# A mixture-of-experts kernel: both products of an expert in matmul pairs of 64 rows, and other rules for the list scheduler

## The chip, the cores and the metric

The kernel runs on one core of a Trainium2 chip. The metric is the time of one execution on the device, in microseconds; of several executions the median counts. TensorE multiplies (its weight loads are listed apart, as PEld), VectorE (DVE) and ScalarE (ACT) compute elementwise, GpSimd (POOL) issues the indirect DMAs, SyncE (SP) issues the other DMAs.

## What is computed

A causal convolution with 7 taps, whose weights are a softmax for each of 8 heads, runs over `x` of 8 x 3584 x 192. Its output rows, 28672 tokens of 192, go through a layer of 8 experts, of which each token takes the two with the largest noisy logits:

```python
logits = x @ w_gate
noise_scale = np.log1p(np.exp(x @ w_noise))
noisy_logits = logits + noise_scale * noise
top2 = np.argpartition(-noisy_logits, 2, axis=1)[:, :2]
...
h = np.maximum(x[mask] @ w1[e], 0.0)
out[mask] += top2_w[mask, k, None] * (h @ w2[e])
```

`w1` is 192 x 1024 and `w2` 1024 x 192 for each expert; the weights of the two experts are a softmax over their two logits. All is float32.

## The kernel before

The tokens are worked on in 28 units of 1024 (8 for each of 128 partitions). For a unit, `conv` makes the convolution on VectorE (56 instructions `tensor_scalar` and `scalar_tensor_tensor`, L560 and L562; for the first five units TensorE does it, L514), scales the rows by a power of two and splits each number into two float16, high and low part, in the tile `rb`. `gating` computes the logits with 24 small matmuls (L637), picks the two experts on VectorE, ranks the tokens of each expert with two more matmuls (L721, L723) or nine in the first units, and `scatters` writes each row to its place in its expert's region of a buffer `xs` in DRAM, by 16 indirect DMAs of GpSimd (L768).

The experts then work in rounds: the first takes 128 rows of each expert, the other 28 take 256. So there are 232 blocks, 224 of them with 256 rows. Each block is loaded by two transposing DMAs into `bT` (three buffers). The first product (`mm1`, L848) has its result, 1024 x 256, in two halves `ph` of two PSUM banks each (two buffers). As the operands are pairs of float16, a product is high x high, high x low and low x high. The rows 128 to 191 of the 192 fill only 64 rows of TensorE. High and low part of these stand side by side on 128 partitions for two of the three products; for the third, low weight with high data, `mm1` runs matmuls of 64 rows, two at a time, on the two halves of the array. For each half that makes 16 matmuls of 128 rows and 4 of 64. Half 0 has its short ones last, half 1 first:

```python
todo = full + todo if half == 0 else todo + full
```

`relu` (ScalarE, L854) writes the high part of the result to `h`, `relu_low` (VectorE, L858) its low part, after which the banks are free. The second product (`mm2`, L866) runs for the block ahead, in two halves of 128 rows with 24 matmuls each, into `py` (one bank each, two buffers). `scaled` (ScalarE, L872) multiplies by the gate, and `add_rows` (GpSimd, L877) adds the rows to the output by an indirect DMA, once the adds of the block ahead have landed.

The order of the instructions on each engine is fixed when the program is built. Each task is a generator that yields an engine and a number of microseconds, and `Plan.run` always takes the task with the smallest `at - urge`, where `at` is the time at which it could start by the plan's own clock. `Ring` holds the number of free buffers, `Mark` makes a task wait for another. `due(u)` says when a unit must be scattered by the plan. `ready_unit` says how many units must be scattered before a round's rows are there: the mean number of rows less 3 standard deviations. The engines run their queues strictly in this order; what they wait for is set by semaphores.

## Time and profile before

| | us |
|---|---|
| median of three runs | 2117.39 |
| the three runs | 2103.3, 2119.4, 2117.39 |
| the profiled execution | 2097.99 |
| its span, first to last instruction | 2096.2 |
| in it: TensorE busy | 1983.7 |
| VectorE busy | 1565.0 |
| GpSimd busy | 1271.8 |
| ScalarE busy | 803.3 |

The profile shows one execution. Busy times of engines overlap, so they don't add up to the span. A line number is one of the kernel. In the timeline a row is a stretch of like instructions on one engine: start and length in microseconds, what is written from what, how many, and in brackets how long the engine was idle ahead of it and what ended that. "issue" is a time in which it waited for nothing that the profile shows. A matmul's length is from its start to its modelled end; matmuls overlap, so the rate is read from the starts.

### The profile page before, as it was taken

The page shows a single profiled execution, that of the slowest core. Times are in us where ns is not written, and L with a number is a line of the kernel's source. Part 1 is how long each engine was busy: PE and PEld are TensorE (multiplying, and loading weights), DVE is VectorE, ACT ScalarE, POOL GpSimd, SP SyncE. Part 2 cuts the span into 40 slices and gives each one's busy share as a digit, 9 for nine tenths or more (in the row PEclk, how much of TensorE's full clock was granted, in tenths as well). Part 3 has the DMA queues.
Part 4 walks back from the last instruction along what each step waited for, and adds up shares of the span by engine and source line. Part 5 has one row for each costly group of instructions (what it writes and reads, how often), then busy time and mean ns, then how long its engine had stood idle before and what let it go on. Part 6 is the DMA issues. An engine that isn't in the chain of part 4 may idle for free.

```text
span 2096.2 us, 52494 instructions
## 1 busy us (share of the span) xinstructions
PE 1983.7 (95%) x21703; PEld 1778.0 (85%) x21703; DVE 1565.0 (75%) x4042; ACT 803.3 (38%) x1173; POOL 1271.8 (61%) x915
## 2 busy tenths in 40 slices
PE   7557999999999999999999999999999999999997
PEld 6546888878888899889899998988898888999986
DVE  6677888878888898889988888889899753333232
ACT  4334343333334343443343434433443433333332
POOL 0353576765666776777667777777767665333333
PEclk9778999999999999999999999999999999999999
DMA  8733456876657677666777766677777664444442
GB/s 238 196 91 79 86 98 118 155 148 118 117 92 125 130 132 128 122 126 117 118 129 133 126 130 117 113 120 131 130 132 115 107 98 77 58 61 57 60 58 35
DMA packets 521882, 236.99 MB, mean 113 GB/s; under 512 B 401304, under 2 KB 508824, under 8 KB 521505
## 3 DMA queue, kind: packets, MB, share of 16 engines
q1 hardware_dynamic: 433824, 142.72, 33.2%
q0 software_dynamic: 87200, 90.80, 29.3%
q8 instruction: 171, 2.80, 0.6%
q14 instruction: 79, 0.65, 0.1%
q10 hardware_dynamic: 608, 0.02, 0.0%
HBM read 40.12 MB, written 115.38 MB: 74 GB/s over the span
## 4 chain that ended last, share of the span: by engine, by line
PE 88%; DVE 5%; issue 3%; SPq 2%; ACT 1%; DMA 1%; another core or an unknown queue 0%; ACTq 0%; POOL 0%; DVEq 0%; POOLq 0%
PE ph L848 43%; PE py L866 41%; PE ph L514 1%; SPq L622 1%; PE misc L637 1%; DVE h L858 1%; PE grams L364 1%; DVE xc L562 0%; DMA xT<-rb 0%; DVE w1s L412 0%; SPq L911 0%; DVE w2s L412 0%; PE py L613 0%; DVE t L673 0%
## 5 line engine op out<-in xcount | busy, mean ns | idle before, releaser
L877 POOL DMA_INDIRECT out_dram<-y,ids x456 | 776.0, 1702 | 593.2 <-ACT y L872 423.5
L848 PE MATMUL ph<-bT,w1s 128*128 128x256 f16 (+2 forms) x9280 | 1004.7, 273 | 26.6 <-issue 10.3
L866 PE MATMUL py<-w2s,h 128*128 128x192 f16 x10944 | 953.1, 246 | 12.0 <-issue 11.3
L848 PEld LDWEIGHTS <-w1s 128*128 128x128 f16 (+1 forms) x9280 | 773.2, 98 | 210.6 <-issue 116.6
L866 PEld LDWEIGHTS <-h 128*128 128x128 f16 x10944 | 910.0, 98 | 23.8 <-issue 18.3
L858 DVE SCALAR_TENSOR_TENSOR h<-ph,h 128x1024 f16<-128x1024 f32 (+1 forms) x464 | 557.5, 1203 | 389.8 <-ACT h L854 345.2
L854 ACT ACTIVATE h<-ph 128x1024 f16<-128x1024 f32 (+1 forms) x464 | 468.0, 1009 | 556.8 <-PE ph L848 469.1
L768 POOL DMA_INDIRECT xs<-rb,idx x448 | 494.2, 1103 | 212.7 <-issue 144.7
L562 DVE SCALAR_TENSOR_TENSOR xc<-xt,wt,xc 128x192 f32<-128x192 f32 x1224 | 422.9, 410 | 3.3 <-DMA xt<-zero 3.3
L872 ACT ACTIVATE y<-py,ga 128x192 f32<-128x192 f32 x456 | 191.5, 421 | 602.2 <-PE py L866 439.2
L514 PE MATMUL ph<-xt,dg 128*128 128x192 f32 x280 | 50.8, 339 | 14.9 <-DMA xt<-in_x_dram 11.6
L514 PEld LDWEIGHTS ph<-xt,dg 128*128 128x128 f32 x280 | 47.3, 197 | 15.3 <-DVE dg L494 11.5
L560 DVE TENSOR_SCALAR xc<-xt,wt 128x192 f32<-128x192 f32 x204 | 53.9, 330 | 1.2 <-DMA xt<-in_x_dram 0.5
L575 DVE TENSOR_REDUCE am<-xc 128x8 f32<-128x1536 f32 x28 | 49.0, 1752 | 4.4 <-ACT xc L569 3.7
L579 DVE TENSOR_TENSOR xc<-xc,xs 128x1536 f32<-128x1536 f32 x28 | 49.3, 1761 | 0.0
L637 PE MATMUL misc<-gparts,xT 128*128 128x32 f16 (+1 forms) x752 | 27.4, 175 | 16.7 <-issue 15.3
L673 DVE SCALAR_TENSOR_TENSOR t<-t,t 128x64 f32<-128x64 f32 x168 | 38.1, 227 | 5.7
L637 PEld LDWEIGHTS <-xT 128*128 128x128 f16 x752 | 24.4, 97 | 19.8 <-issue 17.6
L589 DVE TENSOR_TENSOR rb<-xc,rb 128x1024 f16<-128x1024 f32 x28 | 34.1, 1217 | 4.3 <-ACT rb L585 2.1
L585 ACT ACTIVATE rb<-xc 128x1024 f16<-128x1024 f32 x28 | 29.5, 1053 | 11.1 <-DVE xc L579 9.3
L483 ACT ACTIVATE xt<-xt 128x1152 f32<-128x1152 f32 x27 | 31.2, 1156 | 0.0
L719 DVE TENSOR_REDUCE sums<-M 128x72 f16<-128x576 f16 x23 | 27.0, 1172 | 0.0
(142 smaller groups left out, 620.0 us busy)
## 6 DMA issues: line engine op xcount, KB each, us to landing
out_dram<-zero SPq DMA_DIRECT2D x28, 768.0 KB
xt<-in_x_dram SPq DMA_DIRECT2D x27, 768.0 KB
bT<-xs SPq DMA_TRANSPOSE x464
out_dram<-y,ids POOLq DMA_INDIRECT x456
xs<-rb,idx POOLq DMA_INDIRECT x448
w2s<-in_moe_w_dram SPq DMA_DIRECT2D x16, 384.0 KB
w1s<-in_moe_w_dram SPq DMA_DIRECT2D x8, 512.0 KB
w1s<-in_moe_w_dram SPq DMA_DIRECT2D x16, 256.0 KB
```

The source lines that it names most:

```text
L514: nc.tensor.matmul(c[:, h - h0, :TU * G].rearrange("p (t g) -> p t g", g=G), diag[h, k], xts[u][:, k:k + TU, h * G:(h + 1) * G], start=(k ...
L560: V.tensor_scalar(dst, src, wt[:, h, k:k + 1], None, op0=OP.mult)
L562: V.scalar_tensor_tensor(dst, src, wt[:, h, k:k + 1], dst, op0=OP.mult, op1=OP.add)
L579: V.tensor_tensor(xc, xc, xsc[:, :, None].to_broadcast([P, TU, D]), op=OP.mult)
L637: nc.tensor.matmul(lg[:, t], xT[:, t, c, :], g[:, gc], start=(i == 0), stop=(i == len(seq) - 1))
L768: s = nc.gpsimd.indirect_dma_start(out=xsf, out_offset=bass.IndirectOffsetOnAxis(ap=idx[:, k, t:t + 1], axis=0), in_=rbf[:, t, :], in_offs ...
L848: nc.tensor.matmul(ph[:, f, :T], w, x, start=f // 2 not in banks[:i], stop=f // 2 not in banks[i + 1:], skip_group_check=True)
L854: nc.scalar.activation(h[:, 0, half * nf:(half + 1) * nf, :T], ph[:, :, :T], AF.Relu)
L858: V.scalar_tensor_tensor(h[:, 1, hs, :T], ph[:, :, :T], 0.0, h[:, 0, hs, :T], op0=OP.max, op1=OP.subtract)
L866: nc.tensor.matmul(py[:, :D], h[:, a, f, ts], w2_part(e, lo, f), start=(n == 0), stop=(n == 3 * FC - 1))
L872: nc.scalar.activation(y, py[:, :D], AF.Copy, scale=gate)
L877: a = nc.gpsimd.indirect_dma_start(out=out, out_offset=bass.IndirectOffsetOnAxis(ap=ids, axis=0), in_=y, in_offset=None, compute_op=OP.add)
```

## The change

Both products are cut into matmuls of 64 rows. One on rows 0 to 63 and one on rows 64 to 127 form a pair that writes two different banks. `mm1_pairs` makes two passes over a half: in the first, rows 0 to 63 add to the first bank and rows 64 to 127 to the second, in the second pass (`swap`) the other way round. The matmuls which had 64 rows before are part of the first pass. `mm2_pairs` does the same with the two halves of 128 rows of a block. The first pass has 20 matmuls for each half of the first product, the second 16; the second product has 48 in each pass. `passes` puts a no-op on ScalarE that waits for the last matmul of a first pass, and the first matmul of the second pass waits for it.

The order of a block's work on TensorE is now: first pass of the first product, both halves; first pass of the second product for the block ahead; second pass of the first product, both halves; second pass of the second product for the block ahead. Both `py` banks are held through it. Rounds of 128 rows keep `mm2` as it was.

The scheduler counts 0.3 us more for what follows TensorE (`DRAIN`), and when the best task leaves its engine idle till then, it takes another that ends before (the loop over `able`). Numbers of the plan change: `ready_unit` takes 2.2 standard deviations, the logits of units from the sixth on are planned 5.0 us after their transposes (2.5 before), a scatter takes 1.4 us and an add 2.0, and scatters are due 5 us earlier.

```diff
+    DRAIN = 0.3
...
+                gap = 0.0 if th[4] == eng else self.GAP + (self.DRAIN if th[4] == "PE" else 0.0)
+                at = max(self.clock[eng], th[0] + gap)
...
+            for one in able:
+                if one[2][1][0] == best[2][1][0] and one[1] + one[2][1][1] <= best[1]:
+                    if one[0] < best[0] or one[1] < best[1]:
+                        best = one
...
-            if mean * (u + 1) - 3.0 * sigma * math.sqrt(u + 1) >= end:
+            if mean * (u + 1) - 2.2 * sigma * math.sqrt(u + 1) >= end:
...
-                yield plan.now + 2.5
+                yield plan.now + 5.0
...
-                yield DVE, 0.7
+                yield DVE, 1.1
                 sums = small.tile([P, TU + 1, E], F16, name="sums")
...
+                yield plan.now + 1.0
                 yield PE, 0.1
...
-            yield POOL, 1.05
+            yield POOL, 1.4
...
-            slack = (due(u) - 40.0 - plan.now) / (2 * TU - i)
+            slack = (due(u) - 45.0 - plan.now) / (2 * TU - i)
             if u > 1:
-                yield plan.now + min(2.0, max(0.0, slack - 1.0))
+                yield plan.now + min(2.6, max(0.0, slack - 1.4))
...
+    def passes(what, mm):
+        yield ACT, 0.1
+        passed[what] = nc.scalar.nop()
+        needs(passed[what], mm)
+        done("passed", what, mm.ins.name)
+
+    ROWS = [slice(64 * i, 64 * i + 64) for i in range(2)]
+
+    def mm1_pairs(e, xT, T, half, swap, ph):
+        nf = FC // 2
+        bank = [(f, f + nf // 2) if not swap else (f + nf // 2, f) for f in range(nf // 2)]
+        todo = []
+        for fs in bank:
+            for lo, wc, c in [(0, 0, 0), (1, 0, 0), (0, 0, 1), (0, 1, 2)]:
+                todo += [(f, w1_part(e, wc, lo, half * nf + f)[r], xT[r, c, :T]) for f, r in zip(fs, ROWS)]
+            if not swap:
+                todo += [(f, w1_part(e, 1, 1, half * nf + f)[r], xT[r, 2 + i, :T])
+                         for i, (f, r) in enumerate(zip(fs, ROWS))]
+        for i, (f, w, x) in enumerate(todo):
+            mm = nc.tensor.matmul(ph[:, f, :T], w, x, start=not swap and i < 2, stop=swap and i >= len(todo) - 2,
+                                  skip_group_check=True)
+            if swap and i == 0:
+                needs(mm, passed["ph"])
+        return mm
+
+    def mm2_pairs(e, h, swap, pys):
+        todo = [(i, f, a, lo) for f in range(FC) for a, lo in ((0, 0), (0, 1), (1, 0)) for i in range(2)]
+        for n, (i, f, a, lo) in enumerate(todo):
+            t = 1 - i if swap else i
+            mm = nc.tensor.matmul(pys[t][:, :D], h[ROWS[i], a, f, t * P:(t + 1) * P], w2_part(e, lo, f)[ROWS[i]],
+                                  start=not swap and n < 2, stop=swap and n >= len(todo) - 2, skip_group_check=True)
+            if swap and n == 0:
+                needs(mm, passed["py"])
+        return mm
...
-            for half in range(2):
-                yield PE, 0.1 + 1.96 * T / BIG, ph_ring
+                yield PE, 1.09 * T / BIG, ph_ring
+                phs.append(psum.tile([P, FC // 2, BIG], F32, name="ph", bufs=2))
...
+                mm = mm1_pairs(e, xTs[n], T, half, False, phs[half])
+            plan.spawn(passes("ph", mm), 1.5)
+            if n:
+                yield from second(n - 1, False)
+            yield mark("passed", "ph", mm.ins.name)
+            for half in range(2):
+                yield PE, 0.88 * T / BIG
+                mm1_pairs(e, xTs[n], T, half, True, phs[half])
+                plan.spawn(evacuate(n, half, phs[half], T), 1.5)
...
-                yield from second(n - 1)
-        yield from second(len(blocks) - 1)
+                yield from second(n - 1, True)
+        for swap in (False, True):
+            yield from second(len(blocks) - 1, swap)
```

What this does to the order of the instructions is shown at three places. On VectorE, in the middle of the program, the low parts of `h` (from `ph`) before stood one at a time between steps of the convolution (`xc`):

```order
L858 SCALAR_TENSOR_TENSOR h<-ph,h 128x1024
L562 SCALAR_TENSOR_TENSOR xc<-xt,wt,xc 128x8x24 x11
L858 SCALAR_TENSOR_TENSOR h<-ph,h 128x1024
L562 SCALAR_TENSOR_TENSOR xc<-xt,wt,xc 128x8x24 x2
L858 SCALAR_TENSOR_TENSOR h<-ph,h 128x1024
L562 SCALAR_TENSOR_TENSOR xc<-xt,wt,xc 128x8x24 x14
L858 SCALAR_TENSOR_TENSOR h<-ph,h 128x1024
```

In the same stretch of a later unit they now stand in pairs, one pair for each block, here too with the convolution between them:

```order
L567 TENSOR_SCALAR xc<-xt,wt 128x8x24
L903 SCALAR_TENSOR_TENSOR h<-ph,h 128x1024 x2
L567 TENSOR_SCALAR xc<-xt,wt 128x8x24 x7
L569 SCALAR_TENSOR_TENSOR xc<-xt,wt,xc 128x8x24 x11
L903 SCALAR_TENSOR_TENSOR h<-ph,h 128x1024 x2
L569 SCALAR_TENSOR_TENSOR xc<-xt,wt,xc 128x8x24 x17
L903 SCALAR_TENSOR_TENSOR h<-ph,h 128x1024 x2
```

What stood in two places of a block, 11 or 14 steps and 2 more, now stands in one, 17 or 18 steps.

On ScalarE, where a unit's gating (`t`, `lgs`) falls among the blocks, before:

```order
L854 ACTIVATE h<-ph 128x1024 x2
L872 ACTIVATE y<-py,ga 128x192
L641 ACTIVATE lgs<-misc 128x128
L662 ACTIVATE t_19894<-t_19894 128x64
L872 ACTIVATE y<-py,ga 128x192
L854 ACTIVATE h<-ph 128x1024 x2
```

And now, where the no-ops are not among the rows:

```order
L899 ACTIVATE h<-ph 128x1024 x2
L917 ACTIVATE y<-py,ga 128x192 x2
L648 ACTIVATE lgs<-misc 128x128
L669 ACTIVATE t_32533<-t_32533 128x64
L899 ACTIVATE h<-ph 128x1024 x2
```

The two results `y` of a block now stand together, and the gating stands behind them.

On TensorE, at the change from the second product to the first, with what an instruction waits for, before:

```order
L866 LDWEIGHTS h
L866 MATMUL py<-w2s_144,h 128x192
L848 LDWEIGHTS w1s_130 [waits DMAHW6_49]
L848 MATMUL ph<-bT,w1s_130 128x256 [waits DVE_49]
L848 LDWEIGHTS w1s_130
```

And now, at the change from the first pass of the second product to the second pass of the first:

```order
L891 LDWEIGHTS h
L891 MATMUL py<-w2s_152,h 128x192
L881 LDWEIGHTS w1s_136 [waits Activation_sequencer_49]
L881 MATMUL ph<-bT,w1s_136 128x256
L881 LDWEIGHTS w1s_136
```

Here a wait for ScalarE's no-op is new; the wait for VectorE stands at the first pass of each half.

More of the change, by code (lines that the diff above doesn't have):

```diff
@@ L92, in run @@
         while True:
-            best = None
+            best, able = None, []
             for th in self.threads:
@@ L97, in run @@
                 eng = th[1][0]
-                at = max(self.clock[eng], th[0] + (self.GAP if th[4] != eng else 0.0))
+                gap = 0.0 if th[4] == eng else self.GAP + (self.DRAIN if th[4] == "PE" else 0.0)
+                at = max(self.clock[eng], th[0] + gap)
                 if len(th[1]) > 2:
@@ L104, in run @@
                 urge = th[3](at) if callable(th[3]) else th[3]
+                able.append((at - urge, at, th))
                 if best is None or at - urge < best[0]:
-                    best = at - urge, at, th
+                    best = able[-1]
             if best is None:
@@ L850, in mm1 @@
         return ph
+    passed = {}
+    def passes(what, mm):
[29 more added lines that the diff above has]
+        return mm
     def relu(ph, T, half, h):
@@ L916, in round_meta @@
     def round_meta(j, mt):
-        yield plan.now + 2.3
+        yield plan.now + 4.0
         if j:
@@ L952, in results @@
             yield mark("added", n - 1)
-        yield POOL, 1.6
+        yield POOL, 2.0
         add_rows(j, ids[:, e, half:half + 1], y, adds)
@@ L956, in results, with second @@
         if half == rounds[j][1] // P - 1:
-            done("added", n, after=2.5)
-    def second(n):
+            done("added", n, after=2.8)
+    def second(n, swap):
         j, e = blocks[n]
-        for half in range(2):
-            yield mark("h", n, half)
-        adds = []
-        for half in range(rounds[j][1] // P):
-            yield PE, 2.0, py_ring
-            plan.spawn(results(n, half, mm2(e, hts[n], half), adds), 0.5)
-        hts.pop(n)
+        if swap and rounds[j][1] == P:
+            return
+        if not swap:
+            for half in range(2):
+                yield mark("h", n, half)
+        h = hts[n] if rounds[j][1] == BIG and not swap else hts.pop(n)
+        if rounds[j][1] == P:
+            yield PE, 2.0, py_ring
+            plan.spawn(results(n, 0, mm2(e, h, 0), []), 0.5)
+            return
+        if not swap:
+            pyt[n] = []
+            for half in range(2):
+                yield PE, 2.0 * half, py_ring
+                pyt[n].append(psum.tile([P, 512], F32, name="py", bufs=2))
+        else:
+            yield mark("passed", "py", turn["py"])
+            yield PE, 2.0
+        mm = mm2_pairs(e, h, swap, pyt[n])
+        if not swap:
+            turn["py"] = mm.ins.name
+            plan.spawn(passes("py", mm), 1.5)
+        else:
+            adds = []
+            for half, py in enumerate(pyt.pop(n)):
+                plan.spawn(results(n, half, py, adds), 0.5)
+    pyt = {}
     def run_blocks():
@@ L975, in run_blocks @@
             at_block[:] = n, max(plan.now, FIRST)
-            hts[n] = None
+            phs = []
             for half in range(2):
-                yield PE, 0.1 + 1.96 * T / BIG, ph_ring
+                yield PE, 1.09 * T / BIG, ph_ring
+                phs.append(psum.tile([P, FC // 2, BIG], F32, name="ph", bufs=2))
                 if half == 0:
                     hts[n] = ffn[0].tile([P, 2, FC, BIG], F16, name="h")
-                plan.spawn(evacuate(n, half, mm1(e, xTs[n], T, half), T), 0.6)
+                mm = mm1_pairs(e, xTs[n], T, half, False, phs[half])
[3 more added lines that the diff above has]
+            yield mark("passed", "ph", mm.ins.name)
+            for half in range(2):
+                yield PE, 0.88 * T / BIG
+                mm1_pairs(e, xTs[n], T, half, True, phs[half])
+                plan.spawn(evacuate(n, half, phs[half], T), 1.5)
             xTs.pop(n)
```

## The prediction

> **What bounds the kernel now.** I read the page first: busy shares, granted clock, chain of work.
>
> ```profile
> span 2096.2 us, 52494 instructions
> PE 1983.7 (95%) x21703; PEld 1778.0 (85%) x21703; DVE 1565.0 (75%) x4042; ACT 803.3 (38%) x1173; POOL 1271.8 (61%) x915
> ...
> PEclk9778999999999999999999999999999999999999
> ...
> PE 88%; DVE 5%; issue 3%; SPq 2%; ACT 1%; DMA 1%; another core or an unknown queue 0%; ACTq 0%; POOL 0%; DVEq 0%; POOLq 0%
> PE ph L848 43%; PE py L866 41%; PE ph L514 1%; SPq L622 1%; PE misc L637 1%; DVE h L858 1%; PE grams L364 1%; DVE xc L562 0%; DMA xT<-rb 0%; DVE w1s L412 0%; SPq L911 0%; DVE w2s L412 0%; PE py L613 0%; DVE t L673 0%
> ```
>
> TensorE holds 88% of the chain, nearly all in the two products, at full clock after the start. How close one block is to the rate of the array is read from the timeline, in the last stretch, where VectorE has little else to do.
>
> ```profile
> 2014.29 1.71 PEld L848 LDWEIGHTS <-w1s 128*128 128x128 f16 x16
> 2014.37 4.31 PE L848 MATMUL ph<-bT,w1s 128*128 128x256 f16 x40
> 2014.83 0.42 ACT L872 ACTIVATE y<-py,ga 128x192 f32<-128x192 f32 x1 [1.82 <-PE py L866]
> ...
> 2016.21 0.33 PEld L848 LDWEIGHTS <-w1s 64*128 64x128 f16 x8 [0.21 <-issue]
> 2016.65 1.02 ACT L854 ACTIVATE h<-ph 128x1024 f16<-128x1024 f32 x1 [1.39 <-issue]
> 2016.75 1.64 PEld L848 LDWEIGHTS <-w1s 128*128 128x128 f16 x16 [0.21 <-issue]
> 2017.70 1.22 DVE L858 SCALAR_TENSOR_TENSOR h<-ph,h 128x1024 f16<-128x1024 f32 x1 [4.81 <-ACT h L854]
> ...
> 2018.51 4.12 PE L866 MATMUL py<-w2s,h 128*128 128x192 f16 x48
> ...
> 2018.71 1.02 ACT L854 ACTIVATE h<-ph 128x1024 f16<-128x1024 f32 x1 [1.04 <-PE ph L848]
> 2019.77 1.22 DVE L858 SCALAR_TENSOR_TENSOR h<-ph,h 128x1024 f16<-128x1024 f32 x1 [0.84 <-ACT h L854]
> ...
> 2022.47 4.31 PE L848 MATMUL ph<-bT,w1s 128*128 128x256 f16 x40
> ```
>
> A block takes 2022.47 - 2014.37 = 8.10 us: 4.14 us for the first product, 3.96 us for the second. A slot of the second is 3.96/48 = 82.5 ns. Of the 16 weight loads in 1.71 us the first step is such a slot and the last takes its own 0.098 us; the 14 steps between them are 0.109 us each. The first product has 32 full matmuls and 8 of 64 rows which run two at a time, so 36 slots: 36 x 0.109 = 3.93 us. The missing 0.21 us stands in the two rows with [0.21 <-issue]: the weight loads stop where 128-row matmuls give way to 64-row ones, and again on the way back. So a block is bound by the array, and its only hole is the two changes of row mode.
>
> Then the waits of TensorE after the start, and the two loads that share its time in the middle:
>
> ```profile
> PE ph L848 <- issue: 10.3, 25, 1.2
> PE py L866 <- issue: 9.7, 23, 1.2
> PE misc L721 <- DVE sums L719: 2.2, 3, 1.3
> PE misc L637 <- DMA xT<-rb: 1.2, 2, 0.9
> ...
> 1200.00:1600.00 400.00, 397.69 (x4432) 357.63 (x4431) 354.96 (x938) 158.63 (x233) 285.93 (x204) 1.00 0.71 122
> 1600.00:1900.00 300.00, 298.09 (x3269) 269.15 (x3268) 146.38 (x303) 109.79 (x157) 163.16 (x119) 1.00 0.55 85
> ```
>
> From 200 us on TensorE waits for another engine hardly at all, but 20 us go in 48 short pauses for which the profile names no cause. VectorE (third figure) is busy 89% of the time up to about 1600 us, and half of it after.
>
> **The change, part by part.**
>
> *The pairs.* Every matmul becomes two of 64 rows on the two halves of the array, in different banks. A block then has 72 + 96 matmuls instead of 40 + 48, but in 36 + 48 slots as before, if a pair takes one slot. For that there are rows: from the first of the eight 64-row loads above to the next full one are 2016.75 - 2016.21 = 0.54 us, four slots of 0.109 us and one change of 0.1, so two of them share a slot. With half the columns or fewer, in the first blocks and the gating, the supply was tried harder:
>
> ```profile
> 163.17 0.50 PEld L848 LDWEIGHTS <-w1s 64*128 64x128 f16 x11 [0.17 <-issue]
> 44.14 1.16 PE L637 MATMUL misc<-gparts,xT 128*128 128x16 f16 x40
> ```
>
> Eight 64-row loads and three full ones in 0.50 us, and 40 matmuls with their loads in 1.16 us (29 ns each), are well over the two per 82.5 ns which the second product will ask for. So I price a slot as now, and the gain is the two mode changes: 8.10 - 36 x 0.109 - 48 x 0.0825 = 0.21 us in each of the 224 blocks of 256 rows, 48 us. In the first eight blocks, of 128 rows, the second product stays in 128-row mode, so they gain nothing.
>
> *New mode changes.* The gating's logits (24 matmuls) and its ranks (2) stay in 128-row mode and now stand between 64-row ones: for 23 of 28 units two groups, two changes each, 0.107 us a change: 9.8 us. The first five units have transposes too, about ten groups within the blocks: 2 us. Together +12 us.
>
> *The hand-over.* A second pass adds onto the banks that the other half of the array has just written, so its first load waits for a ScalarE no-op that waits for the first pass. Between the passes of the first product stand 24 slots of the second (1.98 us), and between those of the second the 16 slots of the first (1.75 us). ScalarE's longest operation here is 1.02 us, so the no-op is covered; queued behind it are only the evacuations, which need the second pass anyway. Cost 0; without cover it would be about 0.5 us a pass.
>
> *The evacuation comes closer.* Now each half's banks are needed again 6.0 us after its last matmul (the other half and all of the second product lie between). After the change the first product ends in its second passes, and only half of the second product follows before the banks are needed. From the rows: ScalarE starts 2018.71 - 2018.51 = 0.20 us after the next phase, VectorE 1.06 us later, and ends 1.22 us after that: 2.48 us. Half 0 has 8 x 0.109 + 1.98 = 2.85 us, so 0.37 us to spare. Half 1 queues behind half 0 on both engines and is done 3.63 us after half 0's last matmul; it is needed at 2.85 + 1.09 = 3.94: 0.31 us to spare. Whatever VectorE still has in hand when the ReLU is done comes off that. So what stands ahead of each pair of evacuations must fit into 7.89 us less the pair: the second frees VectorE at 2.41 + 1.14 = 3.55 us, the next pair starts at 7.89 + 1.26 = 9.15, which leaves 5.60 us, and 5.9 us with the spare. Of these the row of 14 gives the price of the filling work:
>
> ```profile
> 1252.38 1.23 DVE L858 SCALAR_TENSOR_TENSOR h<-ph,h 128x1024 f16<-128x1024 f32 x1 [0.21 <-ACT h L854]
> 1253.52 0.74 DVE L562 SCALAR_TENSOR_TENSOR xc<-xt,wt,xc 128x192 f32<-128x192 f32 x2
> ...
> 1255.59 4.69 DVE L562 SCALAR_TENSOR_TENSOR xc<-xt,wt,xc 128x192 f32<-128x192 f32 x14
> ...
> L562 DVE SCALAR_TENSOR_TENSOR xc<-xt,wt,xc 128x192 f32<-128x192 f32 x1224 | 422.9, 410 | 3.3 <-DMA xt<-zero 3.3
> ```
>
> (4.69 - 0.41)/13 = 0.33 us a step. The new order puts 17 such steps between two pairs at most: 5.6 us, just inside. The gating's groups reach about 6.2 us, but in blocks that TensorE's logits lengthen by 0.9 us. So VectorE fits by a hair; for waits inside the gating's chain I take 4 us over the run. The ends: -3.4 us, if the later logits and ranks remove the waits for L719 and the transposes, and 0.5 us in each of the 160 blocks with VectorE's work, 80 us.
>
> *Start and end.* By the order, VectorE gets 30 more convolution steps (10 us) and some routing, 18 us in all, ahead of block 16. It is busy 74 of 100 us there, as this row shows, so most fits into holes; I take +3 us, ends -5 and +18.
>
> ```profile
> 100.00:200.00 100.00, 62.11 (x695) 53.37 (x693) 74.07 (x205) 38.45 (x52) 46.29 (x39) 0.75 0.31 72
> ...
> 2084.40 1.56 POOL L877 DMA_INDIRECT out_dram<-y,ids  x1 [2.75 <-ACT y L872]
> 2086.26 1.56 POOL L877 DMA_INDIRECT out_dram<-y,ids  x1 [0.30 <-issue]
> ```
>
> At the end the last block's adds wait 2.75 us for the adds of the block ahead, not for TensorE; with both halves finishing together that wait stays. 0 us.
>
> *The pauses.* TensorE's instructions nearly double. Were the 20 us tied to their number, they would double too. But the same view from 730 us on, where two thirds of the instructions run, has 1.4 us of them left:
>
> ```profile
> PE ph L848 <- issue: 1.2, 5, 0.3
> PE py L866 <- issue: 0.2, 1, 0.2
> ...
> q8 instruction: 171, 2.80, 0.6%
> ```
>
> I take +3 us, ends 0 and +20. [...]
>
> *GpSimd, the slack of the list scheduler, the earlier readiness (2.2 for 3.0 sigma).* GpSimd is busy 286 of 400 us and off the chain; its own numbers only set where adds and scatters stand. Block loads wait for free buffers, not for scatters. 0 us, hidden by TensorE.
>
> **The sum.** -48 + 12 + 4 + 3 + 0 + 3 = -26 us. The profiled execution took 2098.0 us (span 2096.2 and 1.8 around it): 2072. But the three timed runs shown took 2103.3, 2117.4 and 2119.4, so that execution is the lowest of four, 19 us under the median. The mean of the four is 2109.5; less 26 gives 2084.
>
> **The rivals.**
>
> *A: the evacuation closes the loop, slower.* VectorE's queue is in order. If its work, or a wait in the gating, overruns the 0.31 us by 0.5 us in each of the 160 loaded blocks, TensorE loses 80 us: 2084 - 4 + 80 = 2160. It decides from 0.22 us a block (36 us net gain over 160 blocks); 1% slower from 0.36. For it speaks VectorE's 89% and that the old order kept 3.5 us of cover where the new one keeps 0.3; against it that steps on VectorE take the same time throughout.
>
> *B: the pauses follow the instruction count, no change.* 20 us more from 200 us on and as much as that again ahead of it is not excluded: 2084 - 3 + 20 = 2101, up to 2109 with a slow start.
>
> *C: supply.* TensorE must take 24 matmuls a us for milliseconds; the 40 above were a burst after which the queue could refill. If only the rate of today is sustained, 82.5 ns each, a block takes 168 x 0.0825 = 13.9 us and the kernel 3.4 ms; any rate between is possible, and the bursts are nearer. [...] No run here shows more than 40 in a row.
>
> **How the numbers follow.** About 1% (21 us) is what a measurement of this kernel can tell from no change. My forecast, 0.52: faster by more than 1%, as only the new waits above 5 us more would spoil it. B and mixtures that end within 1%: 0.31. A: 0.14. C: 0.03. The range leaves out A and C, and takes in the full 48 us and a better start from the fastest execution (2098 - 48 - 5 = 2045), and at the top B with the late start and some waits (2119 - 26 + 17 + 15 = 2125, taken as 2130).
>
> **What would show it.** In the timeline after, no [0.21 <-issue] inside a block, and blocks of 7.9 us in the last stretch; if they are 8.1, the pairs don't remove the hole. Among the waits, TensorE on VectorE's h stays under some 15 us in all; 50 us or more there is A. Issue pauses of 40 us instead of 20 are B. Slots over 90 ns in the second product are C. The forecast is wrong too if the first 16 blocks end more than 15 us later.

## The result and the profile after

The changed kernel takes 2267.57 us (four runs, 2257.89 to 2276.01), the kernel before 2114.63 in the same comparison (2103.3 to 2119.4). The ratio is 1.073, 95% interval 1.066 to 1.080: slower by 153 us, where 26 us less were forecast. The profiled execution took 2262.55 us.

Of the page after: the span, the busy shares, and the clock that was granted to TensorE in 40 slices.

```profile
span 2260.8 us, 88992 instructions
PE 2039.0 (90%) x39879; PEld 1900.0 (84%) x39879; DVE 1561.9 (69%) x4042; ACT 763.6 (34%) x1173; POOL 1310.1 (58%) x915
PEclk9677999999999999999999999999999999999999
```

VectorE is busy 3 us less than before, ScalarE 40 us less and GpSimd 38 us longer. TensorE's granted clock is 0.98 from 200 to 2080 us, where it was 1.00 before; between 200 and 800 us it is 0.95 against 0.99. TensorE is busy 90% instead of 95%. Its matmuls are 1.84 times as many. The last stretch shows what the pairs do when nothing disturbs them:

```profile
2104.11 2.08 PEld L891 LDWEIGHTS <-h 64*128 64x128 f16 x48
2106.11 2.20 PEld L881 LDWEIGHTS <-w1s 64*128 64x128 f16 x40
2108.27 1.77 PEld L891 LDWEIGHTS <-h 64*128 64x128 f16 x41
...
2110.31 0.27 PEld L891 LDWEIGHTS <-h 64*128 64x128 f16 x7 [0.27 <-issue]
```

48 loads of the second product take 2106.11 - 2104.11 = 2.00 us, 41.7 ns each, so a pair takes 83 ns; 40 of the first take 2.16 us, 54 ns each, a pair 108 ns. So in this stretch a pair takes one slot, as priced, and no change of row mode stands inside the block. But there is a pause of 0.27 us for which the profile names no cause. The waits of TensorE after 200 us (engine, line, what it waited for: us in total, times, longest) show how many of those there are:

```profile
PE py L891 <- issue: 69.5, 186, 1.1
PE ph L881 <- DVE h L903: 25.3, 52, 1.5
PE ph L881 <- issue: 18.9, 49, 1.1
PE misc L644 <- issue: 5.2, 8, 1.2
```

The 20 us of pauses before have become 94 us, mostly in the second product, and TensorE now waits 25 us for VectorE's part of `h`. These rows count only the time after the modelled end of the last matmul. Read from the starts (every step of more than 0.3 us between consecutive weight loads or matmuls for which no cause is named, after 200 us) the pauses are 38.7 us in 71 places before, and 172.5 us in 305 after. The difference, 134 us, is most of the 165 us between the two profiled executions. (Counted by what the profile names for the instruction behind each step, the pauses are 38.3 and 168.0 us, 130 us apart.)

### The profile page after: what moved, and what is told of

Read it like the earlier page. It is cut to its first block, busy times and chain, and to the rows that moved or that the text cites. A ratio compares the mean times of both kernels' runs of the same rounds, so it can differ in the third digit from the quotient of the medians.

```text
span 2260.8 us, 88992 instructions
## 1 busy us (share of the span) xinstructions
PE 2039.0 (90%) x39879; PEld 1900.0 (84%) x39879; DVE 1561.9 (69%) x4042; ACT 763.6 (34%) x1173; POOL 1310.1 (58%) x915
## 5 line engine op out<-in xcount | busy, mean ns | idle before, releaser
L922 POOL DMA_INDIRECT out_dram<-y,ids x456 | 795.2, 1744 | 700.0 <-ACT y L917 558.4
L891 PE MATMUL py<-w2s,h 64*128 64x192 f16 x21504 | 1031.1, 244 | 73.9 <-issue 69.5
L881 PE MATMUL ph<-bT,w1s 64*128 64x256 f16 (+1 forms) x16704 | 1033.3, 272 | 67.8 <-DVE h L903 30.0
L891 PEld LDWEIGHTS <-h 64*128 64x128 f16 x21504 | 921.0, 94 | 129.9 <-issue 125.0
L881 PEld LDWEIGHTS <-w1s 64*128 64x128 f16 x16704 | 884.1, 96 | 131.1 <-issue 96.4
L903 DVE SCALAR_TENSOR_TENSOR h<-ph,h 128x1024 f16<-128x1024 f32 (+1 forms) x464 | 542.3, 1202 | 494.9 <-ACT h L899 391.0
L899 ACT ACTIVATE h<-ph 128x1024 f16<-128x1024 f32 (+1 forms) x464 | 448.3, 1007 | 1002.3 <-PE ph L881 908.4
L776 POOL DMA_INDIRECT xs<-rb,idx x448 | 513.2, 1146 | 231.6 <-issue 137.5
L917 ACT ACTIVATE y<-py,ga 128x192 f32<-128x192 f32 x456 | 167.6, 419 | 213.5 <-PE py L891 150.9
L521 PE MATMUL ph<-xt,dg 128*128 128x192 f32 x280 | 50.3, 337 | 17.3 <-DMA xt<-in_x_dram 11.6
L419 DVE SCALAR_TENSOR_TENSOR w1s<-w1s,ws,w1s 128x1024 f16<-128x1024 f32 x16 | 20.6, 1285 | 10.8 <-issue 8.4
```

Source lines behind the costliest of these rows:

```text
L521: nc.tensor.matmul(c[:, h - h0, :TU * G].rearrange("p (t g) -> p t g", g=G), diag[h, k], xts[u][:, k:k + TU, h * G:(h + 1) * G], start=(k ...
L776: s = nc.gpsimd.indirect_dma_start(out=xsf, out_offset=bass.IndirectOffsetOnAxis(ap=idx[:, k, t:t + 1], axis=0), in_=rbf[:, t, :], in_offs ...
L881: mm = nc.tensor.matmul(ph[:, f, :T], w, x, start=not swap and i < 2, stop=swap and i >= len(todo) - 2, skip_group_check=True)
L891: mm = nc.tensor.matmul(pys[t][:, :D], h[ROWS[i], a, f, t * P:(t + 1) * P], w2_part(e, lo, f)[ROWS[i]], start=not swap and n < 2, stop=swa ...
L899: nc.scalar.activation(h[:, 0, half * nf:(half + 1) * nf, :T], ph[:, :, :T], AF.Relu)
L903: V.scalar_tensor_tensor(h[:, 1, hs, :T], ph[:, :, :T], 0.0, h[:, 0, hs, :T], op0=OP.max, op1=OP.subtract)
```

## Experiments

The 18 runs fell into two kinds of conditions, which the kernel before tells apart: on chips 8 and 9 it took 2040 us, on chips 4, 11 and 12 between 2110 and 2119, as in the result. On the first two there are practically no pauses in any kernel: in the eight traces from there no row of TensorE's waits after 200 us is without a cause. Each ratio is against the kernel before on the same chip; I call the two "without pauses" and "with pauses". The times expected of the first four runs (e_order_full, e_first_pairs, e_plan_only, e_relaxed) suppose pauses, and all four ran without.

### Order, planner and pairs apart (without pauses)

**e_order_full**: the changed order and planner, with full matmuls of 128 rows in the passes (the second product cut into two halves of its contraction).

```diff
-                todo += [(f, w1_part(e, wc, lo, half * nf + f)[r], xT[r, c, :T]) for f, r in zip(fs, ROWS)]
+        terms = [(0, 0, 0), (1, 0, 0)] if not swap else [(0, 0, 1), (0, 1, 2)]
+        todo = [(f, w1_part(e, wc, lo, half * nf + f), xT[:, c, :T]) for f in range(nf) for lo, wc, c in terms]
...
+        todo = [(t, f, a, lo) for f in range(FC // 2 * swap, FC // 2 * (1 + swap)) for t in range(2)
+                for a, lo in ((0, 0), (0, 1), (1, 0))]
```

> The changed kernel's order of passes, no-ops and planner, but each pass made of full matmuls of 128 rows (only the ones that were short before stay short), so TensorE has as many instructions as before the change. Rate theory (twice the instructions make TensorE pause and send its completions late): 2100 to 2150 us, issue pauses back to 20 to 50 us from 200 us on. Order theory (evacuations with 0.3 us to spare are what TensorE waits for): 2230 to 2270 us. Planner theory (the new numbers of the list scheduler): 2230 us or more.

2097.62 us, ratio 1.029 (1.025 to 1.032). But in this version the 64-row matmuls stand in two places of a block, so that it has four changes of row mode instead of two. Hence **e_order_full_2**, in which they stand side by side:

```diff
+            todo = todo + short if half == 0 else short + todo
```

> The changed order and planner with full 128-row matmuls and, unlike e_order_full, the short matmuls of both halves side by side, so two changes of row mode a block as before the change. The passes of the second product are its two halves of the contraction. Order theory: as slow against before as the changed kernel is in the same run. Pairs theory (instruction count, alone or with late completions): 0.99 to 1.015, as the kernel before has the same matmuls. If e_order_full lost its 57 us to the two more changes of mode, this kernel gains 45 to 60 us on it.

2055.86 us, ratio 1.008 (1.004 to 1.011). Two changes less in each of 224 blocks are worth 41.8 us, 0.093 us each. (The two ran on chips 9 and 8, where the kernel before took 2039.66 and 2040.95 us.) Against before, the order with the changed planner costs 15 us.

**e_first_pairs**: pairs in the first product only, in the changed order.

> The changed kernel with pairs in the first product alone; the passes of the second product are full matmuls. A block has 120 matmuls instead of 168 (before the change 88). Rate theory: the excess goes with the number, 0.4 of it or less: 2140 to 2200 us. Order theory: 2230 to 2270 us. Planner theory: 2230 us or more.

2096.86 us, ratio 1.029 (1.026 to 1.032): as e_order_full, with the same four changes of mode. It tells nothing more.

**e_plan_only**: the blocks of before in the changed planner.

> The blocks as before the change (full matmuls, old order of a block), with the changed scheduler and all its new numbers. Rate theory and order theory: 2090 to 2130 us, as before the change. Planner theory: 2230 us or more.

2045.51 us, ratio 1.001 (0.997 to 1.005). For the old blocks the planner's numbers are worth nothing there.

**e_relaxed**: all pairs, in an order that leaves each half's banks 1.46 us to spare instead of 0.3. Each half's two passes are kept together, with a pass of the second product between them.

```diff
-            for half in range(2):
-                yield PE, 0.88 * T / BIG
-                mm1_pairs(e, xTs[n], T, half, True, phs[half])
+                if half == 0 and n > 1:
+                    yield from second(n - 2, True)
+                if half == 1 and n:
+                    yield from second(n - 1, False)
...
+                yield PE, 0.88 * T / BIG
+                mm1_pairs(e, xTs[n], T, half, True, ph)
```

> All matmuls in pairs, but the passes in another order: half 0 first pass, second pass of the second product of two blocks ahead, half 0 second pass, half 1 first pass, first pass of the second product of the block ahead, half 1 second pass. By the slots each evacuation then has 1.46 us to spare instead of 0.31. Rate theory: 2220 to 2270 us, with 100 us or more of issue pauses. Order theory: 2060 to 2110 us, waits for VectorE's h under 5 us. Planner theory: 2250 us.

2029.88 us, ratio 0.995 (0.994 to 0.997): slightly faster than before. So without pauses pairs can win a little (0.5%). **after_again** is the changed kernel itself under such conditions, **e_relaxed_2** the same as e_relaxed beside it.

> The changed kernel itself, unchanged, again. In the runs above, the kernel before took 2040 us and showed no pause without a named cause, and a kernel of nothing but pairs (e_relaxed) had none either. If the 7% come from such pauses, and they belong to the conditions of the run: with pauses in the kernel before (20 us or more from 200 us on) the ratio is 1.05 to 1.08 with 150 us or more of pauses; without them it is 0.985 to 1.005, since the sum of the prediction (-26 us) holds. If the order of the passes costs the time (evacuations with 0.3 us to spare), the ratio is 1.04 or more in any run and most of it stands as TensorE waiting for VectorE's h.

> e_relaxed again, beside the changed kernel: all pairs, but each half's banks have 1.46 us to spare where the changed kernel has 0.3. If both late completions and tight evacuations are needed for the loss, this kernel keeps 0.99 to 1.01 where the changed kernel loses 3% or more; if the pauses alone make the loss, it loses as much as the changed kernel; if the run has no pauses, 0.99 to 1.00 again and the changed kernel within 1% of it.

The changed kernel took 2065.04 us, ratio 1.014 (1.010 to 1.019), above the 0.985 to 1.005 that were expected without pauses; e_relaxed_2 took 2031.89 us, ratio 0.996 (0.993 to 0.998). So of the 7% of the result 1.4% stay when the pauses are away. TensorE's waits in the changed kernel:

```profile
PE ph L881 <- DVE h L903: 19.2, 10, 10.6
...
PE py L891 <- ACT y L917: 16.1, 4, 8.2
PE misc L644 <- DMA xT<-rb: 13.5, 13, 2.0
```

and in e_relaxed_2:

```profile
PE misc L644 <- DMA xT<-rb: 10.4, 11, 2.6
...
PE py L891 <- ACT y L917: 3.1, 6, 0.5
...
PE ph L881 <- DVE h L903: 0.5, 1, 0.5
```

The two kernels are 33 us apart, and the waits for `h` and for `y` differ by 32 us. So with pairs the tight order costs some 33 us against the relaxed one: few waits, but long ones. The tight order alone does not make them. Of the next rows the first two are of e_order_full_2, which has the tight order with full matmuls, the others of e_plan_only (after 200 us), which has the order of before:

```profile
PE ph L880 <- DVE h L904: 8.0, 7, 2.5
PE py L891 <- ACT y L918: 6.7, 2, 6.5
...
PE ph L856 <- DVE h L903: 10.8, 7, 5.8
PE py L911 <- ACT y L917: 5.3, 2, 4.8
```

These two wait 15 and 16 us, the changed kernel 35 us, so the change adds some 19 us of such waits to the old blocks. Each figure is of one execution.

### What the planner has to do with it

**e_pairs_oldplan**: the changed blocks, with the planner's numbers and rules of before.

```diff
-    DRAIN = 0.3
+    DRAIN = 0.0
...
-            if mean * (u + 1) - 2.2 * sigma * math.sqrt(u + 1) >= end:
+            if mean * (u + 1) - 3.0 * sigma * math.sqrt(u + 1) >= end:
...
-            yield POOL, 1.4
+            yield POOL, 1.05
```

> The changed blocks with the planner's numbers and rules of before. Planner theory: if the changed planner costs time with pairs, this is over 1% faster than the changed kernel. If the changed planner is what keeps VectorE's work out of the way of the tight evacuations, this is 1% or more slower than the changed kernel, with the difference as waits of TensorE for h. If neither, within 0.7% of it.

2235.7 us without pauses, ratio 1.096 (1.092 to 1.101): 171 us more than the changed kernel on the same chip. VectorE's longest waits and what SyncE waits for ahead of the load `mt` (L791), then a stretch of the timeline:

```profile
DVE idf L810 <- DMA mt<-xs: 164.4, 18, 17.6
...
SPq L791 <- DMA xs<-rb,idx: 168.5, 58, 10.7
```

```profile
963.80 0.96 POOL L771 DMA_INDIRECT xs<-rb,idx  x1 [0.30 <-issue]
...
966.17 1.00 SPq L791 DMA_DIRECT2D mt<-xs  x2
...
970.23 0.19 DVE L810 COPY_PREDICATED idf<-ok,mt 128x16 f32<-128x16 int32 x1 [8.51 <-DMA mt<-xs]
...
971.37 2.35 DVE L898 SCALAR_TENSOR_TENSOR h<-ph,h 128x1024 f16<-128x1024 f32 x2
...
972.63 3.59 PE L876 MATMUL ph<-bT,w1s 64*128 64x256 f16 x34 [8.34 <-DVE h L898]
```

This is one link after the other: a unit's last scatter, then the load `mt` of a round's row numbers, which SyncE issues only once the scatters have landed, then VectorE, which has stood 8.51 us in front of that load, then the two evacuations queued behind it, then TensorE. VectorE waits for this load 18 times in the 29 rounds, 9.1 us each on average. **e_oldplan_ready** changes one number of e_pairs_oldplan, the readiness of the rounds:

```diff
-            if mean * (u + 1) - 3.0 * sigma * math.sqrt(u + 1) >= end:
+            if mean * (u + 1) - 2.2 * sigma * math.sqrt(u + 1) >= end:
```

> e_pairs_oldplan with one number of the changed planner, the 2.2 standard deviations of ready_unit. In e_pairs_oldplan VectorE waits 164 us, some 8.4 us in each round, for the round's small load of row numbers, which SyncE issues only when a unit's scatters have landed; the evacuations are queued behind it, and TensorE waits 151 us for them. Theory that the readiness of the rounds makes that wait: 2060 to 2100 us, VectorE's wait for that load under 30 us. Rival, that the planned times of scatters and adds make it: 2200 us or more, with the wait as it was.

It ran with pauses, so its 2460.51 us (ratio 1.165, 1.161 to 1.170) can't be held against the numbers expected. But the wait is gone:

```profile
DVE idf L810 <- DMA mt<-xs: 13.2, 6, 4.8
```

and TensorE's wait for `h` fell from 151.0 to 11.6 us. That the readiness made the wait is shown. How much of the 171 us it makes is not: TensorE's waits for `h` are 132 us longer in e_pairs_oldplan than in the changed kernel on the same chip, and the rest is not taken apart. Why e_oldplan_ready has 323 us of pauses, more than any other with these blocks, is open.

### The pauses

**e_start** is e_relaxed with the blocks of before, full matmuls in their order, up to block 15. **before_again** is the kernel before, on the same chip.

```diff
+    PLAIN = 16
...
+            for half in range(2) if n < PLAIN else ():
+                yield PE, 0.1 + 1.96 * T / BIG, ph_ring
...
+                plan.spawn(evacuate(n, half, mm1(e, xTs[n], T, half), T), 0.6)
```

> e_relaxed, but the first 16 blocks have the full matmuls and the order of before the change. e_relaxed was 19 us behind the kernel with before's blocks (and the changed planner) at the end of its first four blocks and 23 us at the end of the 16th. Theory that the pairs' order makes the start late: 15 to 22 us faster than e_relaxed, ratio 0.985 to 0.989. Rival, that the lost time is caught up again later since VectorE and the scatters set the middle: within 6 us of e_relaxed.

> The kernel before, unchanged, for its own profile under these conditions (2040 us in the runs above, 2115 us in those of the result). If its lower time there is due to the pauses that it lacks, TensorE's pauses without a named cause are under 5 us after 200 us instead of 20 us, and the mean step of a second-product matmul between 200 and 800 us is 82 to 84 ns instead of 85 to 91.

e_start took 2265.4 us, ratio 1.073 (1.070 to 1.076): as much as the changed kernel, with an order that has the time to spare. before_again took 2109.62 us, with 49.6 us of pauses. TensorE's waits in e_start (after 200 us):

```profile
PE py L891 <- issue: 119.0, 296, 1.3
PE ph L881 <- issue: 19.6, 57, 1.0
```

The second product (L891) asks for 24 matmuls a us and the first (L881) for 18, and they take about the same time of a block. Six times as much is lost at the faster one. By the starts e_start has 239.2 us of pauses; the 190 us more than in before_again, less the 45 us that the pairs gain, are 145 of the 152 us between the two profiled executions. Why it has more of them than the changed kernel (172.5 us) is open. What runs beside a pause shows in the timeline of e_start:

```profile
997.78 0.98 POOL L776 DMA_INDIRECT xs<-rb,idx  x1 [0.30 <-issue]
998.36 0.45 PEld L891 LDWEIGHTS <-h 64*128 64x128 f16 x9
...
999.07 0.96 POOL L776 DMA_INDIRECT xs<-rb,idx  x1 [0.30 <-issue]
...
999.26 0.17 PEld L891 LDWEIGHTS <-h 64*128 64x128 f16 x4 [0.45 <-issue]
999.98 0.22 PEld L891 LDWEIGHTS <-h 64*128 64x128 f16 x6 [0.55 <-issue]
...
1000.87 1.18 PEld L891 LDWEIGHTS <-h 64*128 64x128 f16 x29 [0.67 <-issue]
```

Two scatters of GpSimd stand one behind the other; in their time TensorE gets its loads in lumps of 4, 6, then all the rest. Over the whole run this is the rule in the kernels with pairs in the second product; in the kernel before, the pauses lie at scatters hardly more often than the share of the time would give. A table from the traces: pauses from 200 us to the last scatter, how many begin within 1.4 us of a scatter's start, and what share of the time these 1.4 us make, each counted in full.

```
kernel           pauses   within 1.4 us of a scatter   share of the time
before               71    31                            37%
after               297   214                            33%
e_start             397   352                            32%
e_start_full2       141    96                            33%
e_oldplan_ready     498   438                            26%
after the last scatter: before 0, after 8 (3.3 us), e_start 2 (0.7 us)
```

In e_start 239 of the pauses follow the one ahead by less than 1 us; the median from start to start is 0.73 us, and mostly 4 or 5 loads run between. So where TensorE pauses at a scatter it gets some 6 loads and as many matmuls a us. This is not a fixed rate that a scatter leaves over, as the next table shows. It takes the scatters between 800 and 1600 us whose first 1.4 us lie wholly within one product, what that product asks for, and the loads that TensorE started in this time:

```
kernel, product          asked a us   scatters   loads a us   scatters with a pause
before, second               12          119        12.0              2
e_start_full2, second        12           42        11.2              4
e_start_full2, first         18           51        14.6             19
e_start, first               18           29        15.0             11
after, second                24           34        12.6             26
e_start, second              24           75         9.4             69
after_again, second          24           37        24.0              0
```

In the runs with pauses, at 12 a us one is rare (6 of 161 scatters), at 18 it comes at about every third scatter (30 of 80), at 24 at most of them (95 of 109). At 24 TensorE then gets hardly more, and in e_start less, than the 12 which the old second product gets beside the same scatters. After_again, without pauses, gets all 24.

**e_start_late** plans the logits 8.0 us after their transposes.

```diff
-                yield plan.now + 5.0
+                yield plan.now + 8.0
```

> e_start with the logits planned 8.0 us after their transposes instead of 5.0. With all pairs TensorE waits 9 to 10 us in all for these transposes (13.5 us in the changed kernel, 1 to 2 us with before's blocks). If those waits are on the path: 5 to 10 us faster than e_start. If something else waits in their place (the ranks, later scatters): within 4 us of it.

2248.29 us, ratio 1.064 (1.062 to 1.067), 17 us faster than e_start; but its pauses also fell from 239 to 205 us, so the waits for the transposes are not measured by it.

**e_start_2** repeats e_start, and **e_start_full2** gives it full matmuls in the second product.

```diff
-            mm = nc.tensor.matmul(pys[t][:, :D], h[ROWS[i], a, f, t * P:(t + 1) * P], w2_part(e, lo, f)[ROWS[i]],
+            mm = nc.tensor.matmul(pys[t][:, :D], h[:, a, f, t * P:(t + 1) * P], w2_part(e, lo, f),
```

> e_start again. If before takes about 2110 us here, TensorE pauses as it did (200 to 240 us, 85 to 90% of it within 1.4 us of a scatter's start) and the ratio is 1.065 to 1.08. If before takes about 2040 us, no pauses: then the start theory says 2005 to 2017 us, 0.982 to 0.990, and its rival (the lost start is caught up) 2024 to 2034 us.

> e_start with full matmuls of 128 rows in the second product, so 12 matmuls a us there instead of 24, and pairs in the first product only. Each block has four changes of row mode, some 45 us in all. Rate theory (the queue ahead of TensorE covers an interruption at 12 to 18 matmuls a us and not at 24): in a run with pauses those at the second product fall from 119 us to under 20 us, all pauses are under 70 us, and the time is 2130 to 2170 us. Count theory (pauses in proportion to the instructions that the change adds): some 100 us of pauses, 2190 us or more. Without pauses: 2050 to 2065 us.

e_start_2: 2268.76 us, ratio 1.072 (1.069 to 1.075). e_start_full2: 2214.74 us, ratio 1.044 (1.041 to 1.048). Its waits after 200 us, ahead of them the row of the second product in e_start_2:

```profile
PE py L891 <- issue: 124.8, 315, 1.1
...
PE ph L881 <- issue: 33.5, 76, 1.1
PE ph L881 <- ACTq L864: 17.6, 25, 1.3
...
PE py L891 <- issue: 13.8, 32, 1.0
```

At the second product the pauses fell from 125 to 14 us, as the theory of the rate has it, with pairs in the first product as before; that a queue ahead of TensorE covers an interruption, as the theory puts it, no run shows. A full matmul and a pair take the same slot, 82.5 ns before and 83 ns after, so what is halved there is the number of instructions. All pauses by the starts are 84.9 us, against 238.9 in e_start_2. That is above the 70 us of the rate theory, and the time is above its range and within that of the count theory. I had left out that the first product's pauses would grow (14 to 34 us), and the no-op between the passes, for which TensorE waits 17.6 us. And I had mis-sized the changes of row mode: four in each of 216 blocks, at 0.093 us, are 80 us and not 45 against e_start, which has none there. 154 us less of pauses, 80 us more for the changes and 18 us for the no-op leave 56 us; the two kernels are 54 us apart.

**e_scatter_twice** adds a second scatter behind each, of the same rows into another buffer, from the seventh unit on, and takes the 1.4 us it needs off the plan's slack.

```diff
+            if u > 5:
+                yield POOL, 1.4
+                apart()
+                c = nc.gpsimd.indirect_dma_start(
+                    out=xs2f, out_offset=bass.IndirectOffsetOnAxis(ap=idx[:, k, t:t + 1], axis=0),
+                    in_=rbf[:, t, :], in_offset=None)
...
-            slack = (due(u) - 45.0 - plan.now) / (2 * TU - i)
+            slack = (due(u) - 45.0 - plan.now) / (2 * TU - i) - (1.4 if u > 5 else 0.0)
```

> e_start in which GpSimd follows each scatter, from the seventh unit on, with a second one of the same rows to the same places of another buffer that nothing reads. Scatter theory: in a run with pauses these grow by 60 to 100%, to 380 us or more, and lie at both kinds of scatter alike; the kernel takes 2400 us or more. Rival, that the pauses come from something that only runs at the same time (the convolution, the loads of rows): they stay at 200 to 260 us and lie at the old scatters only. Without pauses: within 2% of e_start, as GpSimd has the time.

2670.42 us, ratio 1.262 (1.259 to 1.265). By the starts there are 416 us of steps, but 107 us of them are 8 steps of 11 to 25 us. Those are waits of another kind: by the view of the waits six are for `rb`, one is for `ga` and one has no cause named. The other 502 steps are 309 us, 30% more than in e_start_2 on the same chip, where 60 to 100% more were expected. Put down to the indirect DMA of GpSimd that began last, if within 1.4 us, the 352 added scatters have 197 pauses with 120 us and the 400 old ones 262 with 160 us; in e_start_2 the 400 have 347 with 210 us. So the pauses lie at the added scatters nearly as often as at the old ones, which speaks against the rival, but they do not grow in proportion. The rest of the time is lost otherwise, by block loads and `rb` that come late:

```profile
PE py L901 <- issue: 160.5, 385, 1.9
PE ph L891 <- DMA bT<-xs: 135.1, 14, 11.9
PE ph L891 <- DVE rb L600: 68.3, 6, 12.8
```

**e_tail** is e_start with `PLAIN = 188`: pairs only in the last 44 blocks, about where the scatters end. **e_tail_2** and **e_start_3** repeat both on a further chip.

> e_start with the blocks of before up to block 187, about where the scatters end, and pairs in the last 44 blocks. If the pauses need the scatters: no pause after them, and 44 x 0.2 = 9 us less than with before's blocks alone, 0.992 to 0.998 with pauses or without. If pairs pause without scatters too: 1.00 to 1.02 in a run with pauses.

> e_tail again. The last 44 blocks gain 0.2 us each, 9 us; the rest of its lead of 20 us came from the changed planner at the start, where before's blocks in that planner had no gain over the whole run without pauses (e_plan_only, 1.0008). So 0.988 to 0.995 with pauses, 0.992 to 0.999 without.

> e_start again. With pauses (before at some 2110 us) 1.065 to 1.08. Without (before at some 2040 us): 2005 to 2017 us, 0.982 to 0.990, if the late start of e_relaxed was on the path; 2024 to 2034 us if it was caught up.

e_tail: 2098.12 us, ratio 0.991 (0.987 to 0.994); e_tail_2: 2094.17, ratio 0.990 (0.987 to 0.993); e_start_3: 2274.65, ratio 1.072 (1.069 to 1.076). So e_tail beats both kernels with pauses, by 1%, but not by its pairs. By ScalarE's operations on `py`, its last 28 blocks take 0.19 us less each than in before_again, 5.2 us, but the first 16 blocks of pairs, during which the scatters still run (the last at 1844 us), lose 5.1 us. The lead is made ahead of them, by the old blocks in the changed planner. Its size is unsure: e_tail was 13.6 us ahead of before_again when the pairs began, but 2.1 us ahead of the first trace of the kernel before. Why that planner helps with pauses and not without (e_plan_only) is open.

Each of these two runs also shows pairs and scatters apart. In e_tail, from 900 us to the first pair at 1718 us, full matmuls have 6 pauses beside 201 scatters; from there to the last scatter, pairs have 17 beside 30 scatters, all 17 within 1.4 us of one; behind the last scatter, pairs have none. In e_tail_2 it is 5 beside 198, 18 beside 30, and none. So in these two runs the pauses of the pairs need the scatters, and beside the scatters it takes the pairs.

All runs of e_start had pauses, so what pairs are worth without them, start mended, was not measured.

## Why the prediction was wrong, step by step

**The pairs, -48 us: right.** A pair takes one slot, 108 and 83 ns. In the last 32 full blocks before the end the changed kernel without pauses takes 7.89 us a block, by the spacing of ScalarE's operations on `py`, against 8.09 to 8.10 us in the kernel before: 0.20 us, 45 us over 224 blocks.

**New mode changes, +12 us: the price was right, a wait was forgotten.** A change is 0.093 us where I had 0.107. But without pauses TensorE waits 13.5 us for the transposes, which it waited 1.2 us for in the trace of before and 1.9 us in e_plan_only.

**The hand-over, 0 us: right.** The changed kernel waits 0.7 us for the no-op without pauses and 3 us with them. The 0.5 us a pass without cover was an estimate of mine that no run shows; in e_start_full2, where TensorE often waited for the no-op, it was 0.7 us on average (17.6 us in 25 waits).

**The evacuation, +4 us: too low.** The regular waits of rival A, half a us in each block, did not come, so the steps of VectorE fitted. What the 0.3 us could not take was the rare long delay: without pauses 19.2 us in 10 waits for `h`, 16.1 us in 4 waits for `y`, 19 us more than the old blocks have in the same planner. I had put ahead of the evacuations only work on VectorE, not what VectorE itself would wait for. In the result the waits for `h` are 25 us in 52 places, between the 15 and 50 us that were to separate forecast and A.

**The start, +3 us: too low.** The first 16 blocks end at 304.7 us instead of 278.3, 26 us later, outside the end of +18. e_start, with the old blocks there, brings it back to 276 to 282 us in three runs. Pauses are not needed for it: after_again ends these blocks 20 us later than e_plan_only (264 against 244 us). So it was the pairs in their new order; the idle time of VectorE, which I took as cover, was not what the start lacked.

**The pauses, +3 us with an end of +20: the step that failed.** They grew by 134 us. I argued that they are not tied to the instructions, since two thirds of these run after 730 us almost without them. That was the wrong test, for it was a test at 12 matmuls a us. What the runs showed in its place: beside a scatter of GpSimd the old second product, at 12 a us, gets through nearly always (2 pauses at 119 scatters), and the new one, at 24, mostly does not (pauses at 26 of 34 scatters in the result, at 69 of 75 in e_start), on the chips where pauses come at all. Rival B had named the pauses, but neither its rule, in proportion to the count (1.84 times the matmuls, 4.5 times the pauses), nor its price of 20 us held. Rival C, supply, was right in kind for 1.5 us at a time: the last blocks, without scatters, keep 24 a us with few pauses (8 in the result, 3.3 us). That a queue fed the burst of 40 was a guess of mine that no run shows. The end of my range should have come from C, not from doubling what was seen: nothing in the trace of before showed 24 a us beside a scatter. What holds the instructions up during a scatter stays open.

One supply can be told apart in the traces, the fetches of code, which are queue q8 of the pages. They rose from 171 to 313, one for some 255 loads and matmuls, while 4 or 5 loads run between two pauses; and of the 397 pauses in e_start 70, or 18%, overlap a fetch, where fetches take 16% of the time. So the supply that failed is hardly that one.

**GpSimd and the planner, 0 us: right for the old blocks (1.001), wrong for the new.** With 0.3 us to spare the old planner costs 171 us more than the new one without pauses; 132 us of that are longer waits for `h`, which go with its readiness. "Block loads wait for free buffers, not for scatters" left out the small load `mt`, which does wait for scatters.

The sum for the profiled executions: pauses +134, start +26, waits for `h` +25, gating some +12 (the price, not measured in this trace), pairs -45 make +152; they are 2262.55 - 2097.99 = 165 us apart. The granted clock (0.98 from 200 to 2080 us, where it was 1.00 before) is not among these terms. Start and pauses overlap a little ahead of the 16th block. So one term decides, and the others are of the size of the 1.4% that the change costs without pauses.

## What to carry to other kernels

When a change makes an engine take more and shorter instructions, its bound may become how many of them can start in a us (in the result, 12.6 loads a us beside scatters where 24 were asked). Look at the pauses without a cause that are there already, ask what runs at their side, and price the change by what it asks for in those moments, not by their mean or by a burst elsewhere.

An order that leaves a few tenths of a us between a producer and its consumer is not priced by steady work alone. Follow what the producer's engine waits for over two or three links (here scatter, small load, VectorE, evacuation): 18 such waits, 164 us of VectorE's time, went with 132 us more of TensorE's waits for `h`, where the pairs gain 45 us.

Measure on more than one chip where it can be had: the same two kernels stood 1.4% apart on one and 7.3% on another.

## What the runs showed of the hardware

- On chips 4, 11 and 12 a scatter of GpSimd (0.98 us long in the rows above) went with fewer instructions on TensorE where 24 matmuls a us were asked: in e_start some 6 loads and as many matmuls a us where it paused, in lumps 0.73 us apart. Where 12 were asked, 12.0 ran in the kernel before. On chip 8 the changed kernel ran at 24 a us beside scatters, and TensorE's waits after 200 us name none without a cause. What differs between the chips is not shown.
- Of the 397 pauses of e_start up to the last scatter 352 begin within 1.4 us of a scatter's start, in or just after the 0.98 us of its row. What in the scatter disturbs TensorE no run here shows.
- Beside adds, the other indirect DMAs of GpSimd, pauses are far fewer. Adds go on to the end, and after the last scatter e_start had 2 pauses. But while the scatters ran, 43 of its pauses began within 2 us of an add's start and apart from a scatter, 5.8 per 100 us of such time, against 66 at scatters and 1.3 with neither. In the kernel before, adds and scatters are alike: 5.4 per 100 us at each, 0.3 with neither.
- VectorE pauses too under such conditions: in the result it stood 102.6 us ahead of its part of `h` with no cause named, 40.4 us in the kernel before, but 0.5 us in the changed kernel without pauses.
